# Choosing the early pass's tokens inside attention, and clamping and signing the weight words on ScalarE

## The chip, the cores and the metric

The kernel runs on one core of a Trainium2 chip, as one launch. The metric is the device time of that launch in microseconds (us). The engines are TensorE (PE, with its weight loads PEld), VectorE (DVE), ScalarE (ACT), GpSimd (POOL) and SyncE (SP); each runs its own list of instructions in order and waits on semaphores where another engine's result is needed.

## The reference, cut to what matters

Three layers follow each other on 2304 tokens of 512 features.

```
scores = q k^T / 8                       # 4 batches x 8 heads, 576 x 576, head size 64
keep scores >= max - tau, softmax, times v        -> x [2304, 512]
logits = x @ w_gate; e = argmax(logits)           # 8 experts, one for each token
out[tokens of e] = gate * relu(x @ w1[e]) @ w2[e] # 512 -> 1024 -> 512
h = out @ w_in;  result = (h - tanh(h)) @ w_out   # 512 -> 2048 -> 512
```

`w_in` and `w_out` arrive as float64, that is as pairs of 32-bit words; the kernel turns them into float32 by operations on the words.

## The kernel before, in words

**Attention** (class `Attn`). A unit is one head of two batches; there are 16 units of 9 steps, 144 steps, one step for 128 rows of scores. `run` writes the order by hand: the tables `PL`, `PFIRST` and `PLAST` give each job a step relative to its unit and one of four phases in the step, and `hooks` lets the next class put jobs at steps counted from the start of the last unit (step 135). In a step PE makes scores, VectorE takes the maximum (L235) and masks (L254), ScalarE takes the exponential (L241) and a half-precision copy (L262), and GpSimd the rest of the split (L266). SyncE then issues a DMA transpose for each three steps (L273), and PE multiplies by v (L298). SyncE also issues the loads of q, k and v (v: L107, L109) and the stores of finished rows. For each pair of heads PE transposes the rows (L557) and adds their part of the logits (L565), and VectorE sums it into `L` (L572, L574). The logits of the first half of the tokens are whole at step 95, those of the second half only after the last unit.

**The early pass.** To have work while the second half is finished, one pass of 240 tokens of the first half's most frequent expert is computed first. `best(0)` takes the argmax, `pick` counts by two matmuls (L609, L610), `pick2` finds the expert, `pick3` builds one-hot columns (9 of them at L653), `pick4` turns them into a table of rows by nine matmuls (L659), `pick5` takes those tokens out of the later lists. All of this stands at steps 9 to 15 of the last unit's count, after the last mask. `wearly` loads that expert's eight weight tiles (L1215), `gather_exp` fetches the 240 rows by two indirect DMAs from GpSimd's queue (L1280), `trans` transposes them on PE (L1239), and `evac` splits them into a high and a low part (L1249 on ScalarE, L1253 on VectorE).

**Routing and the expert passes** (`Mlp.run`, `route`, `plan`). After the last logits `route` sorts all tokens on VectorE, with the early pass's matmuls between its parts. Then come eight passes p = 1 to 8, one for each expert from the fullest-capacity table `CAPS`, of 8 steps each (steps g = 8 to 71). In a step PE makes one block of `h` (L1262), ScalarE applies relu (L1303), VectorE takes the low part (L1304), and two steps later PE multiplies by `w2` (L1323). The PSUM tile of `h` has two buffers. Each weight tile is loaded, cast on ScalarE (`wcast`, L1223) and its remainder taken on VectorE or GpSimd (`wlow`, L1227). `FIRST` names the tiles of pass 1 that are loaded and split before its steps begin.

**The words.** Beside the expert passes, 32 jobs `conv` turn half a tile of `w_in` or `w_out` each into float32 and store it in DRAM. `TB["conv"]` and `TB["cv"]` and the line in `plan` put the parts of job n at steps 8 + 14n/9 plus 0, 4, 5 and 6: `load`, `bits`, `sign`, `store`. `bits` shifts and joins the words on VectorE (L1385, L1387) and, in three jobs of four, compares with a threshold (L1390). `sign` takes the absolute value on ScalarE (L1397); in three jobs of four VectorE then makes the sign (L1401), in the fourth ScalarE makes two sign functions (L1395, L1396) and GpSimd adds them (L1399). GpSimd multiplies (L1403).

**The last layer** has 96 steps (g = 72 to 167) of two groups of matmuls (L1262, L1351) with the tanh expression on ScalarE, VectorE and GpSimd between them.

## Time and profile before

| | before |
|---|---|
| device time, median of 3 runs | 1088.42 us (1088.06 to 1088.99) |
| the profiled execution's own time | 1084.18 us |
| its span | 1081.9 us |
| PE busy | 960.4 us (89%) |
| PE weight loads busy | 871.8 us (81%) |
| VectorE busy | 922.6 us (85%) |
| ScalarE busy | 689.3 us (64%) |
| GpSimd busy | 751.2 us (69%) |
| mean granted TensorE clock | 0.949 of full speed |

Busy time counts an instruction from its start to its end, with any time that it is held up inside. A number in square brackets behind an instruction is the time that its engine was idle before it, with the instruction that ended the idle time. L12 is line 12 of the kernel file; a line can be a helper's.

### The profile page before, as it was taken

The page shows a single profiled execution, that of the slowest core. Times are in us where ns is not written, and L with a number is a line of the kernel's source. Part 1 is how long each engine was busy: PE and PEld are TensorE (multiplying, and loading weights), DVE is VectorE, ACT ScalarE, POOL GpSimd, SP SyncE. Part 2 cuts the span into 40 slices and gives each one's busy share as a digit, 9 for nine tenths or more (in the row PEclk, how much of TensorE's full clock was granted, in tenths as well). Part 3 has the DMA queues.
Part 4 walks back from the last instruction along what each step waited for, and adds up shares of the span by engine and source line. Part 5 has one row for each costly group of instructions (what it writes and reads, how often), then busy time and mean ns, then how long its engine had stood idle before and what let it go on. Part 6 is the DMA issues. An engine that isn't in the chain of part 4 may idle for free. (4 is left out here: it accounts for less than half of the span.)

```text
span 1081.9 us, 20819 instructions
## 1 busy us (share of the span) xinstructions
PE 960.4 (89%) x7349; PEld 871.8 (81%) x7349; DVE 922.6 (85%) x1663; ACT 689.3 (64%) x1284; POOL 751.2 (69%) x656
## 2 busy tenths in 40 slices
PE   4687987887986889999998879999999999999997
PEld 3576876776875888899997878788998989999886
DVE  5899888978996748989999986999988989889894
ACT  5797887987983435455555656676666566656662
POOL 3897886886875055466766677787767767677763
PEclk9698898998897789999999999999999999999999
DMA  6798998998899468778788876320101101000000
GB/s 159 149 218 161 206 209 157 216 210 159 158 171 237 155 196 267 252 258 276 259 282 280 267 247 199 95 76 11 49 8 37 30 20 40 8 30 1 21 10 30
DMA packets 250568, 157.29 MB, mean 145 GB/s; under 512 B 179754, under 2 KB 224188, under 8 KB 250461
## 3 DMA queue, kind: packets, MB, share of 16 engines
q1 hardware_dynamic: 246701, 145.18, 53.5%
q0 software_dynamic: 3312, 10.46, 2.8%
q8 instruction: 59, 0.97, 0.4%
q14 instruction: 48, 0.39, 0.1%
q10 hardware_dynamic: 448, 0.30, 0.1%
HBM read 89.24 MB, written 23.57 MB: 104 GB/s over the span
## 5 line engine op out<-in xcount | busy, mean ns | idle before, releaser
L266 POOL TENSOR_TENSOR e<-em,e 128x1024 f16<-128x1024 f32 (+1 forms) x98 | 158.4, 1617 | 55.8 <-ACT e L262 26.1
L1470 POOL TENSOR_SCALAR tm<-u 128x384 uint8<-128x384 f32 x88 | 129.7, 1474 | 50.7 <-ACT u L1466 50.2
L1262 PE MATMUL h<-xa,w 128*128 128x240 f32 (+6 forms) x816 | 135.7, 315 | 17.1 <-DVE w L1227 9.7
L1262 PEld LDWEIGHTS h<-xa,w 128*128 128x128 f32 x816 | 122.4, 194 | 23.4 <-DVE w L1227 11.6
L241 ACT ACTIVATE e<-sps,n 128x576 f32<-128x576 f32 x144 | 111.1, 771 | 34.3 <-DVE n L235 34.2
L1323 PE MATMUL y<-hbuf,w 128*128 128x240 f32 (+6 forms) x768 | 128.3, 317 | 1.0 <-ACT yo L1326 0.9
L1466 ACT ACTIVATE u<-h 128x384 f32<-128x384 f32 x96 | 47.2, 491 | 116.6 <-PE h L1262 116.4
L1473 DVE SCALAR_TENSOR_TENSOR w<-y,w 128x384 f32<-128x384 f32 x96 | 121.3, 1264 | 0.0
L1227 POOL TENSOR_TENSOR w<-raw,w 128x1024 fp32r<-128x1024 f32 x38 | 99.1, 2608 | 31.4 <-ACT w L1223 31.1
L254 DVE SCALAR_TENSOR_TENSOR em<-sps,n,e 128x576 f32<-128x576 f32 x144 | 116.7, 811 | 4.4 <-ACT e L241 2.9
L1323 PEld LDWEIGHTS y<-hbuf,w 128*128 128x128 f32 x768 | 115.3, 193 | 3.9 <-ACT yo L1326 1.6
L235 DVE TENSOR_REDUCE n<-sps 128x1 f32<-128x576 f32 x144 | 107.2, 744 | 11.1 <-PE sps L227 11.1
L1487 POOL TENSOR_TENSOR gl<-w,gh 128x384 fp32r<-128x384 f32 x83 | 85.4, 1029 | 37.1 <-ACT gh L1486 37.1
L1262 PE MATMUL h<-xk,w 128*128 128x384 f32 x576 | 108.5, 337 | 2.5 <-DVE w L1227 2.2
L1262 PEld LDWEIGHTS h<-xk,w 128*128 128x128 f32 x576 | 101.2, 188 | 7.2 <-DVE w L1227 2.9
L298 PE MATMUL ops<-vh,et 128*128 128x64 f16 (+1 forms) x2240 | 97.0, 201 | 9.9 <-DVE x L304 9.0
L262 ACT CAST e<-em 128x576 f16<-128x576 f32 x144 | 100.4, 698 | 3.0 <-DVE em L254 2.6
L298 PEld LDWEIGHTS <-et 128*128 128x128 f16 (+1 forms) x2240 | 83.3, 106 | 22.4 <-issue 18.7
L227 PE MATMUL sps<-ka,qa 128*128 128x288 f32 x320 | 86.3, 362 | 9.5 <-DVE em L254 5.4
L1223 ACT CAST w<-raw 128x1024 fp32r<-128x1024 f32 x80 | 83.7, 1052 | 15.1 <-DMA raw<-in_moe_w_dram 9.3
L1474 DVE SCALAR_TENSOR_TENSOR w<-y,w 128x384 f32<-128x384 f32 x96 | 79.6, 829 | 10.0
L1351 PE MATMUL y<-w,gh 128*128 128x512 f32 x258 | 81.6, 397 | 1.7 <-POOL w L1227 1.3
(271 smaller groups left out, 2345.7 us busy)
## 6 DMA issues: line engine op xcount, KB each, us to landing
raw<-in_moe_w_dram SPq DMA_DIRECT2D x72, 512.0 KB, 5.5
cv<-in_moe_w_in_dram SPq DMA_DIRECT2D x16, 512.0 KB, 4.8
cv<-in_moe_w_out_dram SPq DMA_DIRECT2D x16, 512.0 KB, 4.7
wscr<-cm SPq DMA_DIRECT2D x32, 256.0 KB, 2.6
raw<-wscr SPq DMA_DIRECT2D x16, 512.0 KB, 4.3
xw<-yT SPq DMA_DIRECT2D x24, 192.0 KB, 2.5
vv<-in_v_dram SPq DMA_DIRECT2D x8, 512.0 KB, 5.3
raw<-in_q_dram SPq DMA_DIRECT2D x6, 576.0 KB, 6.8
```

The lines of the kernel that those rows point to most:

```text
L227: nc.tensor.matmul(ps[:, c, 0:288], lhsT=w[:, o:o + 128], rhs=ka[:, j, 288 * c:288 * c + 288], start=(i == 0), stop=(i == n - 1))
L235: nc.vector.tensor_reduce(out=n[:, 0:1], in_=ps[:, :, 0:288], axis=AX.XY, op=ALU.max, negate=True)
L241: nc.scalar.activation(out=e, in_=ps[:, :, 0:288], func=AF.Exp, bias=n[:, 0:1])
L254: nc.vector.scalar_tensor_tensor(out=self.em[u, g][:, i].rearrange("p (a b) -> p a b", a=2), in0=ps[:, :, 0:288], scalar=n[:, 1:2], in1=e, ...
L262: self.nc.scalar.copy(self.e16[u, g][:, i, 0:S], self.em[u, g][:, i])
L266: eng.tensor_tensor(out=e16[:, r, S + 64:], in0=em[:, r, 0:512], in1=e16[:, r, 0:512], op=ALU.subtract)
L298: nc.tensor.matmul(o[q], lhsT=et[:, base + c, q], rhs=vh[:, a, j, c if c < 5 else c - 5, :], start=(n == 0), stop=(n == len(terms) - 1))
L1227: eng.tensor_tensor(out=l, in0=raw, in1=h.bitcast(F32), op=ALU.subtract)
L1262: self.nc.tensor.matmul(out, lhsT=a, rhs=b, start=(i == 0), stop=(i == len(parts) - 1))
L1323: nc.tensor.matmul(self.ys[d], lhsT=a[:, f % 2, s], rhs=b, start=(f == 0 and i == 0), stop=(f == 7 and i == 2))
L1470: nc.gpsimd.tensor_scalar(out=mk, in0=u, scalar1=RCUT * RCUT, scalar2=None, op0=ALU.is_gt)
L1473: V.scalar_tensor_tensor(out=w, in0=y, scalar=b, in1=w, op0=ALU.add, op1=ALU.mult)
```

## The change

Four things are edited.

1. The hooks `best`, `pick`, `pick2`, `pick3`, `pick4` and `pick5` move from steps 9 to 15 of the last unit to steps -40 to -34, that is steps 95 to 101 of attention. Their PSUM tiles come from attention's one transposing bank (tag `t`), their scratch from attention's SBUF pool; the nine one-hot columns become a job of their own (`pick3b`), the table is copied out of PSUM at once and its last addition (`pick6`) stays at step 12, in front of the gather, which moves from step 14 to 12. `x_exp` and `trans` of the early pass move from step 20 to 15, phase 1, `evac` from step 21 to 15, phase 2. `wearly` stays at step 11 and its eighth tile no longer takes a buffer of the tag `raw`.
2. `FIRST` gets a fourth tile, (2, 0).
3. In `conv` a new part `mag` at step 3 makes the sign of the high word (into a bfloat16 tile) and its absolute value in place, both on ScalarE. `bits` begins with a maximum against the threshold on VectorE, and its compare goes; the sign on VectorE (L1401) and the fourth job's sum on GpSimd (L1399) go. The absolute value of the joined word and GpSimd's product stay.
4. The two threshold constants of the old sign functions go.

```diff
     def pick2(self, T):
...
+        self.li1 = T([128, E, NH])
+        tt(self.li1, self.pre1, inc[:, :, 0:NH], ALU.add)
...
+    def pick4(self):
+        nc = self.nc
+        ps = self.attn.tp.tile([128, 512], F32, tag="t", name="pkt")[:, 0:2]
         for t in range(NH):
             nc.tensor.matmul(ps, lhsT=self.B1[:, t], rhs=self.R1[:, t], start=(t == 0), stop=(t == NH - 1))
+        self.idxf = self.cp.tile([128, 2], F32, name="idxf")
+        nc.vector.tensor_copy(self.idxf, ps)
+
+    def pick6(self):
         self.idx1 = self.cp.tile([128, 2], I32, name="idx1")
-        nc.vector.tensor_scalar(out=self.idx1, in0=ps, scalar1=float(ZR), scalar2=None, op0=ALU.add)
+        self.nc.vector.tensor_scalar(out=self.idx1, in0=self.idxf, scalar1=float(ZR), scalar2=None, op0=ALU.add)
...
-FIRST = [(0, 0), (1, 0), (0, 1)]
+FIRST = [(0, 0), (1, 0), (0, 1), (2, 0)]
...
-        return {(9, 0): [self.open1, lambda: self.best(0)],
-                (10, 2): [lambda: self.pick(self.psum)],
-                (11, 0): [lambda: self.pick2(T()), self.wearly],
-                (12, 0): [self.pick3],
-                (14, 2): [lambda: self.pick4(self.psum), lambda: [self.gather_exp(0, m, NE - 128 if m else 128) for m in range(2)]],
-                (15, 0): [self.pick5],
+        return {(9, 0): [self.open1],
+                (-40, 3): [lambda: self.best(0)],
+                (-39, 2): [self.pick, lambda: self.pick2(Carve(self.attn.one.tile([128, 1024], F32, name="pk")))],
+                (-38, 2): [self.pick3],
+                (-37, 2): [self.pick3b],
+                (-35, 2): [self.pick4],
+                (-34, 2): [self.pick5],
+                (11, 0): [self.wearly],
+                (12, 0): [self.pick6, lambda: [self.gather_exp(0, m, NE - 128 if m else 128) for m in range(2)]],
+                (15, 1): [lambda: self.x_exp(0), lambda: [self.trans(("e", 0, m), NE - 128 if m else 128) for m in range(2)]],
+                (15, 2): [lambda: [self.evac(("e", 0, m), 128 * m, NE - 128 if m else 128) for m in range(2)]],
                 (17, 0): [lambda: self.wcast(-1, 0, 0), lambda: self.wlow(-1, 0, 0, self.nc.gpsimd)],
-                (20, 1): [lambda: self.x_exp(0), lambda: [self.trans(("e", 0, m), NE - 128 if m else 128) for m in range(2)]],
                 (21, 0): [lambda: self.wcast(-1, 1, 0)],
-                (21, 1): [lambda: self.wlow(-1, 1, 0, self.nc.vector)],
-                (21, 2): [lambda: [self.evac(("e", 0, m), 128 * m, NE - 128 if m else 128) for m in range(2)]]}
+                (21, 1): [lambda: self.wlow(-1, 1, 0, self.nc.vector)]}
...
-                raw = sp.tile([128, 1024], F32, tag="we" if j and i < 3 else "raw", name="raw", bufs=4)
+                raw = sp.tile([128, 1024], F32, tag="we" if j else "raw", name="raw", bufs=4)
...
+        def mag():
+            st["sg"] = self.sp.tile([128, 512], BF16, tag="gh", name="sg", bufs=LY + 1)
+            nc.scalar.activation(out=st["sg"], in_=st["hf"], func=AF.Sign)
+            nc.scalar.activation(out=st["hf"], in_=st["hf"], func=AF.Abs)
+
         def bits():
             m = st["m"].bitcast(U32)
-            nc.vector.tensor_scalar(out=m, in0=st["hi"], scalar1=3, scalar2=0x40000000,
+            nc.vector.tensor_scalar(out=st["m"], in0=st["hf"], scalar1=T, scalar2=None, op0=ALU.max)
+            nc.vector.tensor_scalar(out=m, in0=m, scalar1=3, scalar2=0x40000000,
                                     op0=ALU.logical_shift_left, op1=ALU.bitwise_xor)
             nc.vector.scalar_tensor_tensor(out=st["lo"], in0=st["lo"], scalar=29, in1=m,
                                            op0=ALU.logical_shift_right, op1=ALU.bitwise_or)
-            if not sg:
-                nc.vector.tensor_scalar(out=st["m"], in0=st["hf"], scalar1=-T, scalar2=None, op0=ALU.is_le)
 
         def sign():
             c = st["lo"].bitcast(F32)
-            if sg:
-                nc.scalar.activation(out=st["m"], in_=st["hf"], func=AF.Sign, bias=self.tt2[:, 0:1])
-                nc.scalar.activation(out=st["hf"], in_=st["hf"], func=AF.Sign, bias=self.tt2[:, 1:2])
-            nc.scalar.activation(out=c, in_=c, func=AF.Abs, scale=0.5 if sg else 1.0)
-            if sg:
-                nc.gpsimd.tensor_tensor(out=st["m"], in0=st["m"], in1=st["hf"], op=ALU.add)
-            else:
-                nc.vector.scalar_tensor_tensor(out=st["m"], in0=st["hf"], scalar=T, in1=st["m"],
-                                               op0=ALU.is_ge, op1=ALU.subtract)
-            nc.gpsimd.tensor_tensor(out=st["m"], in0=st["lo"].bitcast(F32), in1=st["m"], op=ALU.mult)
+            nc.scalar.activation(out=c, in_=c, func=AF.Abs)
+
+        def mul():
+            nc.gpsimd.tensor_tensor(out=st["m"], in0=st["lo"].bitcast(F32), in1=st["sg"], op=ALU.mult)
...
-        return [load, bits, sign, store]
+        return [load, mag, bits, sign, mul, store]
...
-                  47, 51, 52, 54, 57, 57), "cv": (0, 4, 5, 6), "eng": "DPDPDPDPDPPDDDPP"}
+                  47, 51, 52, 54, 57, 57), "cv": (0, 3, 4, 5, 5, 6), "eng": "DPDPDPDPDPPDDDPP"}
```

The arithmetic before attention's end, the passes, the routing and the last layer are as they were.

## Rows read from the trace of the kernel before

**Rows 1.** Windows by stage: start:end, length, busy us of each engine, PEclk, DMA, GB/s
```profile
50.00:332.00 282.00, 230.94 (x3085) 205.15 (x3086) 250.39 (x647) 237.21 (x416) 232.51 (x235) 0.92 0.99 187
332.00:392.00 60.00, 49.77 (x455) 47.44 (x455) 37.39 (x123) 19.76 (x34) 18.92 (x20) 0.77 0.62 169
392.00:661.00 269.00, 245.08 (x1635) 233.41 (x1635) 234.40 (x296) 142.80 (x251) 171.38 (x96) 0.98 0.82 267
735.00:1011.00 276.00, 275.65 (x1381) 248.63 (x1381) 245.93 (x348) 171.07 (x360) 200.06 (x161) 1.00 0.07 23
```
**Rows 2.** Windows over attention around steps 95 to 101 and after them
```profile
228.40:239.60 11.20, 10.44 (x141) 9.31 (x141) 10.53 (x29) 11.12 (x21) 9.46 (x10) 0.89 1.09 199
245.10:332.00 86.90, 72.06 (x979) 64.12 (x980) 80.07 (x205) 72.75 (x126) 70.56 (x74) 0.91 0.89 166
```
**Rows 3.** Timeline, VectorE near steps 95 and 101: start, us, what, idle before it
```profile
228.40 0.22 DVE L574 TENSOR_TENSOR L<-L,ops 128x72 f32<-128x72 f32 x1
245.10 0.82 DVE L127 TENSOR_REDUCE pm<-vv 128x1 f32<-128x640 f32 x1 [5.51 <-DMA vv<-in_v_dram]
```
**Rows 4.** Sum over the four windows that hold the early choice on VectorE
```profile
sum 7.67, PE 6.23 PEld 6.02 DVE 7.03 ACT 2.29 POOL 1.53; mean PE 1.56 PEld 1.50 DVE 1.76 ACT 0.57 POOL 0.38
```
**Rows 5.** Timeline of the passage from attention to routing: all engines
```profile
332.07 0.81 DVE L254 SCALAR_TENSOR_TENSOR em<-sps,n,e 128x576 f32<-128x576 f32 x1
334.96 0.28 PE L609 MATMUL y<-O,onesh 128*128 128x152 f16 x1 [5.22 <-DVE O L578]
335.18 0.27 POOL L279 TENSOR_SCALAR su<-su,sc 128x9 f32<-128x9 f32 x1
344.35 2.99 PE L298 MATMUL ops<-vh,et 128*128 128x64 f16 x56
344.98 1.08 POOL L1280 DMA_INDIRECT xr<-rows,idx  x1 [9.53 <-DMA raw<-in_moe_w_dram]
352.83 0.66 PE L1239 MATMUL y<-ident,xr 128*128 128x128 f32 x4 [3.29 <-DMA xr<-rows,idx]
354.68 1.01 PE L1239 MATMUL y<-ident,xr 112*128 112x112 f32 x4 [1.19 <-DMA xr<-rows,idx]
359.92 0.23 DVE L574 TENSOR_TENSOR L<-L,ops 128x72 f32<-128x72 f32 x1 [2.88 <-PE ops L565]
390.37 4.31 PE L1262 MATMUL h<-xa,w 128*128 128x240 f32 x36 [0.45 <-ACT yo L1326]
```
**Rows 6.** Timeline at the start of pass 1: SyncE's loads, ScalarE's cast
```profile
393.59 1.19 SPq L1215 DMA_DIRECT2D raw<-in_moe_w_dram  x2
398.41 1.05 ACT L1223 CAST w<-raw 128x1024 fp32r<-128x1024 f32 x1 [4.67 <-DMA raw<-in_moe_w_dram]
```
**Rows 7.** Windows of pass 1, of passes 4 and 5, of passes 6 and 7
```profile
392.00:421.70 29.70, 25.26 (x186) 24.16 (x186) 20.45 (x48) 13.07 (x25) 13.13 (x8) 0.89 0.88 294
499.60:567.20 67.60, 64.02 (x430) 62.54 (x429) 65.33 (x80) 37.20 (x66) 44.77 (x27) 1.00 0.85 274
567.20:633.80 66.60, 55.23 (x406) 52.22 (x405) 62.23 (x64) 35.48 (x63) 45.09 (x25) 1.00 0.80 265
```
**Rows 8.** Groups of instructions, 392 to 660 us, VectorE: busy us, mean ns, idle before
```profile
L1401 DVE SCALAR_TENSOR_TENSOR cm<-cv,cm 128x512 f32<-128x512 f32 x24 | 31.0, 1292 | 0.0
L1304 DVE SCALAR_TENSOR_TENSOR hbuf<-h,hbuf 128x240 fp32r<-128x240 f32 (+6 forms) x64 | 30.9, 483 | 22.5 <-ACT hbuf L1303 22.3
L1390 DVE TENSOR_SCALAR cm<-cv 128x512 f32<-128x512 f32 x24 | 24.1, 1005 | 0.8
```
**Rows 9.** The same of ScalarE and GpSimd
```profile
L1396 ACT ACTIVATE cv<-cv,knt 128x512 f32<-128x512 f32 x8 | 6.2, 772 | 0.3
L1395 ACT ACTIVATE cm<-cv,knt 128x512 f32<-128x512 f32 x8 | 6.1, 767 | 10.8 <-DVE cv L1387 10.8
L1403 POOL TENSOR_TENSOR cm<-cv,cm 128x512 f32<-128x512 f32 x32 | 45.4, 1419 | 49.8 <-issue 11.4 <-ACT hbuf L1303 11.0 <-ACT w L1223 10.3
L1399 POOL TENSOR_TENSOR cm<-cm,cv 128x512 f32<-128x512 f32 x8 | 11.0, 1370 | 9.7 <-ACT cv L1396 9.7
```
**Rows 10.** Single lines: shortest, median, longest ns, first and last start
```profile
L1401 DVE SCALAR_TENSOR_TENSOR cm<-cv,cm x24: 676/684/3494, 411.9 to 618.6; 128x512 f32<-128x512 f32 x24
L1390 DVE TENSOR_SCALAR cm<-cv x24: 426/428/2800, 410.4 to 616.9; 128x512 f32<-128x512 f32 x24
```

More of the change, by code (lines that the diff above doesn't have):

```diff
@@ L604, in best, with pick @@
         tt(self.O[:, :, 1 + NH * P:1 + NH * P + NH], eq, bt(tm), ALU.is_equal)
-    def pick(self, psum):
+    def pick(self):
         nc = self.nc
-        self.tot1, self.pre1 = psum("y2", [128, E, NTL + 1]), psum("y3", [128, E, NH])
+        n = E * (NTL + 1)
+        t = self.attn.tp.tile([128, 512], F32, tag="t", name="pkp")
+        self.tot1 = t[:, 0:n].rearrange("p (e t) -> p e t", e=E)
+        self.pre1 = t[:, n:n + E * NH].rearrange("p (e t) -> p e t", e=E)
         nc.tensor.matmul(self.tot1, lhsT=self.onesh, rhs=self.O, start=True, stop=True)
@@ L633, in pick3 @@
         n9 = lambda dt=F32: T([128, NH], dt)
-        li, O1 = T([128, E, NH]), T([128, E, NH])
-        loc, loi, lo, h1, vl, tv = n9(I32), n9(I32), n9(), n9(), n9(), n9()
+        li, O1 = self.li1, T([128, E, NH])
+        loc, loi, lo, h1, tv = n9(I32), n9(I32), n9(), n9(), n9()
+        vl = self.cp.tile([128, NH], F32, name="vl")
         A, R, B = T([128, NH, 2]), T([128, NH, 2], F16), T([128, NH, 128], F16)
-        self.O1, self.loc1, self.vl, self.B1, self.R1 = O1, loc, vl, B, R
-        tt(li, self.pre1, self.inc1[:, :, 0:NH], ALU.add)
+        self.O1, self.loc1, self.vl, self.B1, self.R1, self.lo1 = O1, loc, vl, B, R, lo
         tt(O1, O, self.sel1.unsqueeze(2).to_broadcast([128, E, NH]), ALU.mult)
@@ L1073, in run @@
             nc.gpsimd.memset(self.ab[:, i:i + 1], self.kn[2 * i])
-        T = float(np.nextafter(np.float32(3.4332275390625e-05), np.float32(0)))
-        self.tt2 = self.cp.tile([128, 2], F32, name="knt")
-        for i in range(2):
-            nc.gpsimd.memset(self.tt2[:, i:i + 1], T if i else -T)
         self.keep = sp.tile([128, 3072], F32, tag="lxa", name="keep")
@@ L1368, in conv @@
         T = 3.4332275390625e-05
-        sg = n % 4 == 3
         st = {}
```

8 lines of the change are left out of this document (3 added, 5 removed).

## The prediction

> **What bounds the kernel now.** I read the windows by stage first [rows 1]. From 735 to 1011 us PE is busy 275.65 of 276 us at the full granted clock: the last layer is PE's own, and nothing in the change touches it, so it can only begin earlier or later. The reader should look for the stages where PE is not full. There are three. In attention (50 to 332) PE has 231 of 282 us, VectorE 250, ScalarE 237, GpSimd 233, and the DMA engines are at 0.99: everything is near full and VectorE is the fullest of the engines. In the passage from attention to the expert passes (332 to 392) no engine but PE is half busy, the granted clock is 0.77, and the stage is a chain of waits. In the expert passes (392 to 661) PE has 245 of 269.
>
> Second, the windows of single passes [rows 7]. In passes 4 and 5 PE idles 3.6 us of 67.6, in 6 and 7 it idles 11.4 of 66.6, and VectorE is busy 65.3 and 62.2: as the experts' capacity falls, a step of PE becomes shorter than VectorE's work beside it, and VectorE bounds. Pass 1 idles 4.4 of 29.7 with VectorE at only 20.5, so its reason is another.
>
> Third, the groups of instructions there [rows 8, 10]. L1390 takes 0.43 us at the median but 1.0 on the mean and 2.8 at the worst; L1401 0.68, 1.29 and 3.5. L1304, whose one big input lies in PSUM, has 0.48 on the mean for tiles of 240 and more. So much of VectorE's busy time is being held up, and only in instructions that work from SBUF, as GpSimd's do.
>
> Fourth, the timeline of the passage [rows 5]: who ends each idle time, from the last mask to pass 1.
>
> **The change part by part.**
>
> *The choice inside attention.* 39 VectorE instructions move to steps 95 to 101, and one copy is new. In the old place they fill four short windows of 7.67 us together with VectorE busy 7.03 [rows 4]. I price them at 7.67. New are waits of VectorE for the counting matmuls and for the table's nine, and of PE for the shared PSUM bank; the nearest row has VectorE idle 5.51 us for another result, but that is a DMA; PE's queue in attention is nearly full rather than late, so I allow 0 to 1.5 us. Behind these wait the step's mask and, through it, the split and the DMA transpose. The cover: VectorE is busy 10.53 of 11.20 us in the very steps [rows 2], so nothing hides there, but right behind, at step 101, it stands 5.51 us until the loads of v land [rows 3]. Those were issued behind a queue of transposes on SyncE, which the later masks do not reach yet, so they land when they did. 7.67 + 0.5 against 5.51 leaves 2.66; I take 2.5 us lost. Ends: 0 (all in the gap) and 9.2 (the loads move too). From 245 to 332 VectorE is busy 80 of 87 us [rows 2], so what is lost there is hardly made good.
>
> *The passage.* Removed: PE's 5.22 us for the argmax at L609 [rows 5]. It is not all gain. The next thing late is the last head's own chain: GpSimd's L279 at 335.2, which opens the reciprocal on VectorE, then the rows, and with them the PSUM half that PE needs for its next product. PE so gains some 2 us there. Then the gather: idx no longer waits for PE at 344, and GpSimd is free at 335.5, so it is issued some 8 us earlier, near 337. From the first issue to the first transposing took 352.83 - 344.98 = 7.9 us, so rows are there near 345 and 346. The transposes now stand ahead of the products of rows 4 to 8 in PE's order, where PE comes near 343.5: it waits some 2 us there in place of 3.29 + 1.19 later. After them come 84 products, for which 2.99 us for 56 [rows 5] give 4.5 us, and the 4.9 us of logits that stood behind the transposes before (355.0 to 359.9). So the sum of the logits, at 359.92 before, ends near 356: 4 us. Ends: 0 (gather as late as before, counted from the end of attention) and 9.7 (5.22 + 3.29 + 1.19). From that sum to pass 1's first matmul at 390.37 lies the sorting and its gather, 30.5 us, which I leave as they are.
>
> *wearly.* Its place in SyncE's queue is behind the last transpose as before, so its loads start where they did; the eighth no longer waits for a buffer and holds the rows' stores up less, which nobody waits for. Nothing.
>
> *The fourth FIRST tile.* At 393.59 SyncE issues pass 1's loads and ScalarE stands 4.67 us at the first cast with relu behind it [rows 6]. One load of 0.52 MB less in that crowd, at the 294 GB/s of [rows 7], is 1.8 us; its cast (1.05) and remainder go to the stage before, where ScalarE has 19.8 of 60 and VectorE 37.4 [rows 1]. I take 1.5; ends 0 and the stage's whole 4.4.
>
> *The words.* VectorE loses L1401, 24 times; L1390 becomes the maximum, of the same shape and strides, and comes 8 times more often. At mean durations 31.0 - 8 x 1.005 = 23.0 us; at the medians 24 x 0.684 - 8 x 0.428 = 13.0 [rows 8, 10]. GpSimd loses L1399, 11.0 us [rows 9]; its product reads a bfloat16 operand now and I leave it at 1.42. ScalarE gains two functions in 24 jobs, 24 x (0.767 + 0.772) = 36.9 us [rows 9]. The 32 jobs spread over 50 steps, 0.64 a step, so passes 4 to 7 (32 steps) hold 0.64 of all: VectorE 8.3 (medians) to 14.7 us (means), ScalarE +23.6. PE's idle there is 15.0 [rows 7]. ScalarE was busy 72.7 of 134 us in these passes and becomes 96.3 of some 125, so it has room; its new functions stand a step ahead of VectorE's maximum, with a relu between that VectorE needs anyway, so no new wait arises there. But relu can come behind them. I take 8 us, near the medians, and 1 for passes 1 to 3, where PE is nearly full. Ends: 14.7 + 2, and on the other side 14.7 - 23.6 = -9, if every added function stood ahead of a relu that PE waits for.
>
> The Trainium skill (SBUF — State Buffer, section SBUF: two separate sides) calls the port that VectorE and GpSimd share an exclusive lock, held for a whole instruction, against VectorE's two-port modes and its instructions with two SBUF inputs. The longest L1401, 3.5 us, agrees with it. By that rule each held-up time goes with its instruction and GpSimd's 11.0 us come back too, so the words would be worth 14.7 in passes 4 to 7 and up to PE's whole idle; without it 8.3. The full return is my first rival, priced from the rows alone.
>
> **Sum.** -4 + 2.5 - 1.5 - 9 = -12.0 us. The profiled execution took 1084.18 us (span 1081.9 and 2.3 around it), so it would be 1072.2; the median of the runs is 4.24 above the profiled one, and I put the forecast on the median: 1088.4 - 12.0 = 1076.4 us.
>
> **Rivals.**
>
> *A. VectorE gives all of it back.* Passes 4 to 7 lose PE's whole 15.0 us of idle, passes 1 to 3 another 2, the passage 7, pass 1's load 2.5, attention costs 1: -25.5, 1062.9 us. For it: idle before L1401 is 0.0, VectorE never rests [rows 8]. Against: DMA is at 0.80 to 0.85 there [rows 7] and ScalarE fills up.
>
> *B. Moved, not saved.* The choice costs attention its whole 9.2, the passage gives nothing, because the gather lands as late against PE as before; words and load give 9 of their 10.5: +0.2, 1088.6 us. For it: VectorE's 250 of 282 in attention [rows 1]. Against: the 5.51 us gap.
>
> *C. ScalarE's queue, the slower side.* In passes 4 to 7 relu waits behind sign and absolute value, the low part behind relu, and PE behind the low part, since `h` has two buffers. Each job then costs 1.54 us and gives back 0.7: -9 us of gain become 9 of loss, with 3 for the rest: +6, 1094.4 us. It decides once ScalarE's 1.54 us fall between the end of an `h` and its relu in more than about half of the jobs (then the 23.6 us outweigh VectorE's 8 to 15). For it: ScalarE already stands 10.8 us in 8 jobs at L1395 for VectorE [rows 9], and what stands behind stands too. Against: after the change sign comes ahead of the shift and waits only for the load. The Trainium skill (ScalarE: Activation LUTs, section Rules for kernel authors) advises VectorE, not ScalarE, for simple functions; the medians agree with that, 0.77 against 0.43 us for the same tile, and this is the rival that it would lead to.
>
> **How the numbers follow.** Forecast 0.55, A 0.14, B 0.13, C 0.13, and 0.05 for a loss elsewhere (a late tile, a slower first pass). A measurement of this kernel can tell about 0.2%, 2.2 us, from no change. Forecast and A are faster; B splits into 0.03, 0.07 and 0.03; C is slower, and of the rest 0.04. Faster 0.72, same 0.08, slower 0.20. The forecast's own range is 1066 to 1084. All lower ends together would give 1058, all upper ones 1107, which no one case reaches; for 8 in 10 I take 1063 (A) to 1091, which leaves out most of C.
>
> **What would show it.** Attention's last mask, at 332.1 us before [rows 5], 2 to 3 us later, with VectorE's wait for v shortened from 5.5 to under 1. No idle of PE at L609, the gather issued near 337 on the old clock, and pass 1's first matmul at 390.4 + 2.5 - 4 = 389 us. PE's idle in pass 1 near 3 us, in passes 6 and 7 near 5 instead of 11.4, and ScalarE near 0.75 busy there. The last layer's 276 us unchanged. I am wrong if the last mask moves by more than 6 us (B), or if relu's wait for PE's `h` shrinks to nothing while passes 6 and 7 are not shorter (C).

## The result and the profile after

| | before | after |
|---|---|---|
| device time, median of 5 runs each | 1088.06 us (1085.72 to 1088.99) | 1077.96 us (1075.77 to 1079.61) |
| ratio, after to before | | 0.9911, 95% interval 0.9889 to 0.9932 |
| span of the profiled execution | 1081.9 us | 1076.0 us |

The change makes the kernel 10.1 us faster; 12.0 had been forecast, and the forecast time of 1076.4 us lies 1.6 us below the median. The two traces differ by only 5.9 us of span, because the profiled execution of before, at 1084.18 us, was shorter than any of the timed ones (1085.08 to 1091.95 over all comparisons). A trace is one execution: where a difference of one or two microseconds matters, the medians and the experiments decide.

The windows of after that answer to [rows 1, 2, 7], in this order: from the last mask to the last logits, pass 1, passes 4 and 5, passes 6 and 7, the last layer, and in attention from VectorE's sum L574 to the first value tile L127 (columns as in [rows 1]):

```profile
338.42:358.20 19.78, 14.55 (x188) 13.69 (x189) 5.37 (x17) 6.45 (x12) 6.42 (x9) 0.65 1.06 269
390.70:419.10 28.40, 23.70 (x187) 23.06 (x186) 18.41 (x40) 16.67 (x33) 15.36 (x10) 0.94 0.83 282
496.30:560.10 63.80, 63.76 (x432) 62.59 (x431) 52.23 (x74) 46.45 (x82) 38.57 (x24) 1.00 0.87 285
560.10:623.80 63.70, 55.22 (x404) 51.99 (x404) 52.07 (x60) 40.39 (x75) 38.57 (x22) 1.00 0.83 275
729.10:1005.10 276.00, 276.00 (x1381) 249.54 (x1381) 245.02 (x347) 170.94 (x360) 198.18 (x160) 1.00 0.07 23
229.49:251.60 22.11, 16.21 (x152) 14.14 (x153) 21.49 (x68) 11.84 (x21) 10.35 (x11) 0.58 1.00 189
```

Read them against before. The passage took 359.92 - 332.07 = 27.9 us [rows 5] and takes 19.8. Passes 4 to 7 took 134.2 us [rows 7] and take 127.5; in them VectorE was busy 127.6 us and is busy 104.3. PE is now full in passes 4 and 5 and still idles 8.5 us in 6 and 7, where every other engine has room. The last layer is 276 us, as before. The stretch in attention took 245.10 - 228.40 = 16.7 us [rows 3] and takes 22.1. From relu to relu, passes 1 to 7 together went from 241.8 to 233.1 us; of what lies behind them, pass 8 is 2.7 us longer in this trace and the last layer as long as before.

**Attention.** The timeline of after, VectorE, in and behind the choice (columns as in [rows 3]):

```profile
231.06 2.12 DVE L578 TENSOR_TENSOR O<-rt 128x72 f16<-128x72 f32 x1
235.65 0.82 DVE L578 TENSOR_TENSOR pk<-pk 128x8 f32<-128x8 f32 x1
241.74 3.65 DVE L660 TENSOR_SCALAR pk<-i128h,pk 128x128 f16<-128x128 f16 x9
251.60 0.81 DVE L127 TENSOR_REDUCE pm<-vv 128x1 f32<-128x640 f32 x1
```

The window of the same stretch in before (columns as in [rows 1]):

```profile
228.40:245.10 16.70, 11.61 (x159) 10.26 (x158) 10.54 (x30) 11.93 (x22) 12.34 (x13) 0.91 1.11 205
```

Six masks (L254) fall into the stretch before and after, so the difference is the choice. VectorE was busy 10.54 us in it and is busy 21.49: the choice takes 10.95 us of VectorE here. 6.16 us of them are time in which VectorE stood before (16.70 - 10.54), 0.62 us of idle time are left, and the stretch is 5.41 us longer. The granted clock is 0.58 in it, 0.91 before; VectorE is full here, so no cost of that is seen.

The same stretch of GpSimd:

```profile
230.96 2.13 POOL L266 TENSOR_TENSOR e<-em,e 128x1024 f16<-128x1024 f32 x1 [2.04 <-ACT e L262]
235.26 1.20 POOL L266 TENSOR_TENSOR e<-em,e 128x512 f16<-128x512 f32 x1 [0.42 <-ACT e L262]
242.49 2.14 POOL L266 TENSOR_TENSOR e<-em,e 128x1024 f16<-128x1024 f32 x1 [5.77 <-DMA vv<-in_v_dram]
```

Lay the two over each other. O's write starts 0.10 us after a split of GpSimd and ends with it. Nine of the experiments below have this write in attention: in five no split lies beside it and it takes 0.24 us, in four a split does and it takes 1.8 to 1.9. The nine one-hot columns contain one that took 2.13 us, against a median of 0.25; it starts 0.06 us after GpSimd's split from 242.49 to 244.63 and ends with it. L127 no longer waits: the 5.51 us gap [rows 3] is used up whole.

The Trainium skill (SBUF — State Buffer, section SBUF: two separate sides) has it that of VectorE and GpSimd whichever starts first gets the port that they share, and that the loser is blocked for the other's whole instruction. These rows agree for the write of O, the one-hot column and the 128x8 instruction at 235.65: each starts behind a split and lasts until it ends. Not every instruction of VectorE is held up so: a reduction at 235.46 (L581, 128x1 from 128x8) takes 0.16 us inside the split that starts at 235.26.

**The passage.** The timeline of after that answers to [rows 5], all engines:

```profile
338.42 0.81 DVE L254 SCALAR_TENSOR_TENSOR em<-sps,n,e 128x576 f32<-128x576 f32 x1
341.54 0.28 POOL L279 TENSOR_SCALAR su<-su,sc 128x9 f32<-128x9 f32 x1
342.59 0.91 PE L298 MATMUL ops<-vh,et 128*128 128x64 f16 x14 [5.07 <-DVE x L304]
342.91 1.07 POOL L1289 DMA_INDIRECT xr<-rows,idx  x1 [1.10 <-DVE idx L673]
349.41 1.84 PE L1248 MATMUL y<-ident,xr 128*128 128x128 f32 x8
358.20 0.23 DVE L574 TENSOR_TENSOR L<-L,ops 128x72 f32<-128x72 f32 x1
389.01 4.28 PE L1271 MATMUL h<-xa,w 128*128 128x240 f32 x36 [0.49 <-ACT yo L1335]
```

PE no longer waits for the argmax. It waits instead 5.07 us for the rows L304, which stand behind the denominator L279 on GpSimd; for the first half of this time a DMA transpose is late too (a weight load of PE waits for it until 340.03). The gather goes out 4.5 us after the mask, where it was 12.9, and PE does eight transposes in one go, with no wait in front, where [rows 5] had 3.29 and 1.19.

The granted clock has a part in it. These are the windows of the last 18 logits products (L565) with three transposes among them, up to the last sum, before and after:

```profile
355.48:359.92 4.44, 4.44 (x24) 4.44 (x23) 0.69 (x2) 2.02 (x4) 0.00 (x0) 0.50 0.91 264
355.46:358.20 2.74, 2.66 (x22) 2.57 (x23) 1.23 (x2) 2.73 (x4) 0.47 (x3) 1.00 1.06 380
```

Before, PE had stood 3.29 and 1.19 us for the rows just ahead of them and did them at 1.2 GHz (0.50); after, it had not stood there and did them at 2.4 GHz (1.00), 1.70 us faster.

**The words.** Groups of after over 392 to 660 us, VectorE first (columns as in [rows 8]):

```profile
L1399 DVE TENSOR_SCALAR cm<-cm 128x512 uint32<-128x512 uint32 x32 | 39.2, 1224 | 1.1
L1398 DVE TENSOR_SCALAR cm<-cv 128x512 f32<-128x512 f32 x32 | 28.5, 891 | 0.6 <-issue 0.4 <-DMA wscr<-cm 0.2
L1401 DVE SCALAR_TENSOR_TENSOR cv<-cv,cm 128x512 uint32<-128x512 uint32 x32 | 28.2, 880 | 1.1
...
L1394 ACT ACTIVATE cv<-cv 128x512 f32<-128x512 f32 x32 | 21.7, 678 | 1.0
L1393 ACT ACTIVATE sg<-cv 128x512 bf16<-128x512 f32 x32 | 21.4, 669 | 0.0
```

L1399 is now the shift and L1398 the new maximum. Both are still held up: their means are 1.22 and 0.89 us, while their medians are 0.43 and 0.42 and the longest 2.66 and 2.47. The two functions on ScalarE take 0.67 us each, steadily. Who waits for whom in passes 6 and 7 of after (560 to 624 us), as waiter, what ended the wait, us in total, times, longest:

```profile
ACT cv L1406 <- DVE cv L1401: 21.5, 8, 4.2
...
PE h L1271 <- DVE hbuf L1313: 3.9, 4, 1.5
...
PE h L1271 <- DVE w L1236: 2.1, 5, 0.6
...
PE y L1332 <- ACT yo L1335: 1.5, 2, 0.8
```

The last three, with 0.5 us each in front of two transposes, are the whole 8.5 us for which PE stands in these passes: the low part of `h` and weight remainders on VectorE, and ScalarE's copies of finished blocks.

And one such place in the timeline, all engines but SyncE:

```profile
574.62 2.59 POOL L1236 TENSOR_TENSOR w<-raw,w 128x1024 fp32r<-128x1024 f32 x1
...
574.99 2.50 DVE L1399 TENSOR_SCALAR cm<-cm 128x512 uint32<-128x512 uint32 x1
...
577.52 0.69 DVE L1401 SCALAR_TENSOR_TENSOR cv<-cv,cm 128x512 uint32<-128x512 uint32 x1
578.13 0.45 DVE L1313 SCALAR_TENSOR_TENSOR hbuf<-h,hbuf 128x288 fp32r<-128x288 f32 x1
578.25 0.67 ACT L1406 ACTIVATE cv<-cv 128x512 f32<-128x512 f32 x1 [3.95 <-DVE cv L1401]
...
578.63 1.86 PE L1271 MATMUL h<-xa,w 128*128 128x288 f32 x12 [0.66 <-DVE hbuf L1313]
```

A split of GpSimd runs from 574.62 to 577.21. VectorE's shift beside it ends 0.28 us later, after 2.50 us where the median is 0.43; the join and then the low part of `h` follow in VectorE's order, and PE waits for that low part.

### The profile page after: what moved, and what is told of

It is laid out like the page before. It is cut to its first block, busy times and chain, and to the rows that moved or that the text cites. A ratio compares the mean times of both kernels' runs of the same rounds, so it can differ in the third digit from the quotient of the medians.

```text
span 1076.0 us, 20810 instructions
## 1 busy us (share of the span) xinstructions
PE 961.3 (89%) x7349; PEld 872.5 (81%) x7349; DVE 891.3 (83%) x1648; ACT 715.4 (66%) x1332; POOL 733.2 (68%) x646
## 4 chain that ended last, share of the span: by engine, by line
PE 42%; DVE 13%; issue 4%; ACT 3%; DMA 3%; POOL 2%; SPq 0%; POOLq 0%; DVEq 0%; ACTq 0%
PE h L1271 20%; PE y L1360 15%; PE y L1332 6%; DVE w L1479 2%; DVE w L1480 2%; DVE cm L1399 2%; DMA raw<-in_moe_w_dram 1%; DVE cm L1398 1%; DVE w L1236 1%; DVE w L1477 1%; ACT w L1232 1%; DMA wscr<-cm 1%; DVE cv L1401 1%; DVE tm L1478 1%; POOL w L1236 1%
## 5 line engine op out<-in xcount | busy, mean ns | idle before, releaser
L1236 POOL TENSOR_TENSOR w<-raw,w 128x1024 fp32r<-128x1024 f32 x38 | 95.2, 2507 | 73.9 <-ACT w L1232 45.5
L254 DVE SCALAR_TENSOR_TENSOR em<-sps,n,e 128x576 f32<-128x576 f32 x144 | 116.6, 810 | 5.2 <-ACT e L241 3.4
L1332 PEld LDWEIGHTS y<-hbuf,w 128*128 128x128 f32 x768 | 115.2, 193 | 5.4 <-ACT yo L1335 3.1
L235 DVE TENSOR_REDUCE n<-sps 128x1 f32<-128x576 f32 x144 | 107.0, 743 | 10.1 <-PE sps L227 10.0
L1480 DVE SCALAR_TENSOR_TENSOR w<-y,w 128x384 f32<-128x384 f32 x96 | 77.7, 809 | 10.7 <-DVE w L1479 0.9
```

The lines of the kernel that those rows point to most:

```text
L235: nc.vector.tensor_reduce(out=n[:, 0:1], in_=ps[:, :, 0:288], axis=AX.XY, op=ALU.max, negate=True)
L254: nc.vector.scalar_tensor_tensor(out=self.em[u, g][:, i].rearrange("p (a b) -> p a b", a=2), in0=ps[:, :, 0:288], scalar=n[:, 1:2], in1=e, ...
L1236: eng.tensor_tensor(out=l, in0=raw, in1=h.bitcast(F32), op=ALU.subtract)
L1332: nc.tensor.matmul(self.ys[d], lhsT=a[:, f % 2, s], rhs=b, start=(f == 0 and i == 0), stop=(f == 7 and i == 2))
```

## The experiments

Each kernel was timed beside the kernel before on the same chip; ratios are to that.

**The choice alone**: the change without its words and without the fourth FIRST tile.

```diff
-FIRST = [(0, 0), (1, 0), (0, 1), (2, 0)]
+FIRST = [(0, 0), (1, 0), (0, 1)]
 (and conv, its constants and "cv" as in the kernel before)
```

> The early choice moved into attention and the eight weight tiles' buffers as in the change; the words and FIRST as before. Read from the two traces: attention +6.35 us (last mask 332.07 to 338.42), the passage from the last mask to the second half's logits -8.07, so about -1.7 us, 1086 us against a before of 1088. Rival (the whole gain comes from the passage, and attention's later end is this execution's own slowness): -8 us, 1080. Second rival (attention pays more than the passage returns): 1089 or more. In its trace the last mask should come 6 us later than before and the nine one-hot columns of L653's group should take 3.6 us together in place of 1.55, with a write of O of 2 us or more.

Measured: 1084.46 us against 1088.93, ratio 0.9976 (0.9959 to 0.9994). The medians are 4.5 us apart; the ratio and its interval say some 2.6 us faster (0.7 to 4.5), which is near the theory. The passage takes 21.0 us, the stretch in attention 251.06 - 229.71 = 21.4, and passes 4 to 7 are as long as before (134.3). Of the signs in its trace the one-hot columns came (3.66 us); the long write of O did not, since no split lay beside it (0.24 us), and the last mask came 4.7 us later, not 6.

**The words alone**: the kernel before with the new `conv` and nothing else.

```diff
-        return [load, bits, sign, store]
+        return [load, mag, bits, sign, mul, store]
 (mag, bits, sign, mul and "cv" as in the changed kernel)
```

> The words' new parts alone; choice and FIRST as before. The theory (VectorE bounds passes 4 to 7, and what it and GpSimd no longer do comes back there): passes 4 to 7 shorter by 7 to 8 us, all else the same, so 1080 us against 1088. Rival (the gain of these passes needs the earlier start of pass 1 or the fourth FIRST tile): under 3 us. Rival (ScalarE's 37 us more cost passes 1 to 3 what 4 to 7 gain): no change, 1088.

Measured: 1078.28 us, ratio 0.9904 (0.9882 to 0.9926), 10.5 us faster. The whole change has 0.9911. So the words alone do as much as the change, and beside them the 2.6 us of the choice can't be seen: the parts do not add. Passes 4 to 7 of this kernel, to be set beside the two middle rows of after:

```profile
503.10:630.50 127.40, 119.04 (x833) 114.67 (x833) 103.99 (x133) 86.76 (x155) 77.28 (x45) 1.00 0.85 281
```

127.4 us, against 127.5 in the change, with the same busy times: the choice plays no part in the passes. This run also tells how far attention varies. Its attention is the kernel before's, line for line, and its last mask stands at 337.9 us, not at 332.1; 5.1 us of that are there already at L574 (233.53 against 228.40).

**FIRST with three tiles**: the change with that one edit undone.

```diff
-FIRST = [(0, 0), (1, 0), (0, 1), (2, 0)]
+FIRST = [(0, 0), (1, 0), (0, 1)]
```

> The changed kernel with three FIRST tiles in place of four. Theory: the fourth tile gives nothing, because in pass 1 PE then waits 3.9 us for the third gathered block of pass 2's rows instead: within 1 us of the changed kernel, 1078. Rival (my prediction's step): 1.5 us slower, 1079.5. Rival (the fourth tile is what made pass 1 longer): 2 us faster, 1076.

Measured: 1076.49 us, ratio 0.9900 (0.9875 to 0.9924); the change has 0.9911 (0.9889 to 0.9932). No difference that can be told. Pass 1 is 28.7 us with three tiles and 28.4 with four.

**ScalarE's new work twice**: sign and absolute value each made twice in all 32 jobs, with the same values.

```diff
+            nc.scalar.activation(out=st["sg"], in_=st["hf"], func=AF.Sign)
             nc.scalar.activation(out=st["sg"], in_=st["hf"], func=AF.Sign)
+            nc.scalar.activation(out=st["hf"], in_=st["hf"], func=AF.Abs)
             nc.scalar.activation(out=st["hf"], in_=st["hf"], func=AF.Abs)
```

> The changed kernel with the two new ScalarE functions of every job done twice (sign written twice, absolute value taken twice; the result stays): ScalarE gets another 32 x 1.36 = 43 us. Theory (ScalarE has room, at 46.9 of 65.7 us in passes 4 and 5 and 38.5 of 60.6 in 6 and 7): 0 to 6 us slower than the changed kernel, 1078 to 1084. Rival (relu stands behind the new functions and PE behind relu, so each function costs its length in passes 4 to 7): 0.64 x 43 = 28 us slower, 1106.

Measured: 1088.89 us, ratio 1.0010 (0.9990 to 1.0031), 10.9 us above the change. ScalarE's 32 x 1.35 = 43 us of extra work cost a quarter of their length, which neither the theory (0 to 6 us) nor the rival (28) had. In passes 4 to 7:

```profile
499.20:635.00 135.80, 120.75 (x828) 116.26 (x827) 101.10 (x133) 109.87 (x192) 75.44 (x45) 0.97 0.80 264
```

with VectorE's wait for relu grown from 19.1 to 30.1 us, and PE's for ScalarE's copies from 1.5 to 4.2:

```profile
DVE hbuf L1313 <- ACT hbuf L1312: 30.1, 17, 3.3
...
PE y L1332 <- ACT yo L1335: 4.2, 2, 2.2
```

ScalarE is busy 23.0 us more there and the passes are 8.3 us longer, although ScalarE would seem to have had 127.5 - 86.9 = 40.6 us to spare. So the room was smaller than its busy share said. Relu does stand behind the new functions, as rival C had it; but that is not where PE waits. PE idles 15.1 us in these passes, 6.5 more than in the change, and its wait for the low part behind relu is 2.8 us, not more than the 3.9 of the change. What grew is its wait for the copies (by 2.7), for weight tiles, which ScalarE casts first (2.5), and in front of transposes (2.2). At the change's own dose the price of all this stays below what VectorE gives back.

**GpSimd's product twice**: the last product of each job made twice.

```diff
             nc.gpsimd.tensor_tensor(out=st["m"], in0=st["lo"].bitcast(F32), in1=st["sg"], op=ALU.mult)
+            nc.gpsimd.tensor_tensor(out=st["m"], in0=st["lo"].bitcast(F32), in1=st["sg"], op=ALU.mult)
```

> The changed kernel with GpSimd's product of every word job done twice (the result stays): GpSimd gets another 32 x 1.4 = 45 us, 29 of them in passes 4 to 7, where it is busy 76 of 126 us and has room. Theory (VectorE is held up while GpSimd reads SBUF, so what GpSimd does costs VectorE): VectorE's busy time in these passes grows by 10 to 25 us and the kernel takes 8 to 20 us more, 1086 to 1098. Rival (the two run side by side and only instruction lengths of VectorE itself count): 0 to 2 us, 1078 to 1080.

Measured: 1094.78 us, ratio 1.0063 (1.0042 to 1.0084), some 16.8 us above the change for 32 x 1.43 = 46 us more on GpSimd. Passes 4 to 7:

```profile
500.20:637.20 137.00, 120.25 (x833) 115.83 (x832) 115.22 (x133) 86.88 (x156) 106.73 (x66) 0.99 0.82 262
```

The three instructions of the jobs on VectorE, in the same passes:

```profile
L1398 DVE TENSOR_SCALAR cm<-cv 128x512 f32<-128x512 f32 x19 | 25.4, 1335 | 1.6 <-issue 1.4
L1399 DVE TENSOR_SCALAR cm<-cm 128x512 uint32<-128x512 uint32 x19 | 25.3, 1331 | 0.7
...
L1401 DVE SCALAR_TENSOR_TENSOR cv<-cv,cm 128x512 uint32<-128x512 uint32 x19 | 21.1, 1109 | 0.7
```

Nothing was added to VectorE, and it is busy 10.9 us longer (104.3 to 115.2). The three groups together took 63.1 us in the change (19.2, 27.7 and 16.2) and take 71.8. The passes are 9.5 us longer. GpSimd itself is not full, 107 of 137 us. The rival, that a job's product lies beside other work and costs nothing, falls. VectorE is one of two ways in which the product is paid for:

```profile
PE h L1271 <- DVE hbuf L1313: 8.2, 6, 2.5
...
PE t L1248 <- DMA xr<-rows,idx: 4.9, 2, 2.9
```

PE idles 8.2 us more than in the change. Its wait for VectorE's low part grew by 4.3 us, and a wait for gathered rows of 4.9 us is new: GpSimd issues those gathers, in its own order behind the doubled product (for pass 6 at 564.47, 3.2 us ahead of that pass's first relu, where the change has 4.5). So this run shows the hold-up on VectorE, but it does not price it alone.

**The one-hots back behind attention**: everything else of the change kept.

```diff
-        return {(9, 0): [self.open1],
+        return {(8, 3): [self.pick3b],
+                (10, 3): [self.pick5, self.pick4],
...
-                (-37, 2): [self.pick3b],
-                (-35, 2): [self.pick4],
-                (-34, 2): [self.pick5],
-                (11, 0): [self.wearly],
+                (11, 0): [self.open1, self.wearly],
```

> The changed kernel with the one-hot columns (pick3b), the table's matmuls (pick4) and pick5 back behind the last mask, where VectorE and PE stand idle for 2.6 and 5.1 us; argmax, counts and pick3 stay in attention, and the weight tiles' pool opens two steps later. Theory (in attention these cost 3.6 + 0.2 + 1.0 us of VectorE, held up by GpSimd, with nothing to hide them): attention's steps 95 to 102 go from 24.1 back to 19.5 to 20.5 us, the passage stays at 20 to 21: 4 us faster than the changed kernel, 1074. Rival (the cost is the wait for the counting matmuls and the argmax, which stay): under 1 us faster. Rival (PE is late behind the table in the passage): attention 4 us faster, passage 3 us slower, 1077.

Measured: 1074.08 us against 1088.07, ratio 0.9859 (0.9838 to 0.9879), 3.9 us faster than the change, and with the version "Both" below the best of those that were timed. The same stretch of attention (L574 to L127):

```profile
234.41:252.18 17.77, 13.77 (x143) 11.89 (x144) 16.68 (x51) 10.84 (x20) 9.57 (x10) 0.73 0.94 200
```

17.8 us, 4.3 less than in the change and near before's 16.7, though the first half of the choice is still in it. In the passage the one-hots come right behind the last mask:

```profile
338.54 2.83 DVE L660 TENSOR_SCALAR pk<-i128h,pk 128x128 f16<-128x128 f16 x9
...
340.93 0.34 POOL L279 TENSOR_SCALAR su<-su,sc 128x9 f32<-128x9 f32 x1
```

They lie in the time in which PE and VectorE wait for L279 anyway; the passage takes 21.1 us.

**Pass 2's last gather one step earlier**, on the change. In its trace PE stands 3.86 us in pass 1 for the third gathered block of pass 2, whose DMA is issued on GpSimd behind a split that waits for ScalarE.

```diff
-                at(max(g - B["ga"], 8) + m, self.gather_exp, p, m, w)
+                at(max(g - B["ga"], 8) + (min(m, 1) if p == 2 else m), self.gather_exp, p, m, w)
```

> The changed kernel with the third and fourth gathers of pass 2's rows issued by GpSimd one and two steps earlier, ahead of the remainder of a weight tile that GpSimd waits 9.7 us for. Theory (with the fourth FIRST tile in place, PE's 3.9 us wait for these rows in pass 1 is what comes next): pass 1 goes from 28.4 to about 25 us, 3 us faster in all, 1075. Rival (the weight tiles' loads are what pass 1 waits for in any case): under 1 us.

Measured: 1079.86 us, ratio 0.9900 (0.9871 to 0.9928). The wait is gone, and pass 1 is 27.9 us instead of 28.4: what comes next is late as well. No difference can be told in the whole time.

**Both, with the last denominator earlier as well**: the two edits above and `"de": (9, 1)` in `PLAST`, which lets GpSimd sum the last unit's denominator sooner.

```diff
-    PLAST = {"te": (4, 3), ..., "rc": (11, 1), ...
+    PLAST = {"te": (4, 3), ..., "de": (9, 1), "rc": (11, 1), ...
```

> late_onehot and gather_ahead together, and the last head's denominators (L279) on GpSimd one phase earlier, ahead of the last split instead of behind it. Theory: 4 us from attention, 3 from pass 1, and 2 from the passage, since the reciprocal and with it PE's next product wait for L279 at 341.5 with GpSimd idle before: 1069 us. Rival (the parts do not add, since pass 1 then waits for its weight loads): 1073.

Measured: 1072.41 us, ratio 0.9858 (0.9836 to 0.9881), the same as with the one-hots alone, and near the rival's 1073. The third edit was not timed by itself; the timeline says why nothing is seen of it. L279 now runs from 336.01 to 336.35, while VectorE is in the one-hots (L660, from 335.28) until 338.11 and takes the reciprocal only at 339.05. One wait has taken the place of another.

**The absolute value of the joined word one step later**, on the change and on the version with the late one-hots. It is meant to tell ScalarE's queue from VectorE's order, as what still holds PE up in passes 6 and 7.

```diff
-                  47, 51, 52, 54, 57, 57), "cv": (0, 3, 4, 5, 5, 6), "eng": "DPDPDPDPDPPDDDPP"}
+                  47, 51, 52, 54, 57, 57), "cv": (0, 3, 4, 6, 6, 7), "eng": "DPDPDPDPDPPDDDPP"}
```

> The changed kernel with the last absolute value, GpSimd's product and the store of every conversion job one step later; nothing else moves. In passes 4 to 7 of the changed kernel ScalarE stands 25.8 us in 12 places at L1406 for VectorE's join L1401, with relu, sign and casts queued behind, and PE still idles 8.5 us in passes 6 and 7. Theory S (ScalarE's queue sets those idle times): with the step between, ScalarE's wait shrinks to under 8 us, relu is earlier, PE's idle in passes 6 and 7 falls to under 4 us and the time by 4 to 8 us: 1070 to 1074, ratio to before 0.983 to 0.987. Theory V (VectorE's own order sets them: its sum L1313, which PE waits for, stands behind the shift L1399, which takes 2.50 us instead of 0.4 while GpSimd splits): ScalarE's wait shrinks as well, but PE's idle stays within 2 us of 8.5 and the time within 2.5 us of the changed kernel: 1075 to 1080, ratio 0.989 to 0.994.

> The same shift on the version whose one-hots stand after the last mask. By theory S it takes another 4 to 8 us off that version's 1074.1: 1066 to 1070, ratio to before 0.980 to 0.983. By theory V it stays within 2.5 us: 1072 to 1077, ratio 0.984 to 0.989.

Measured: 1078.11 us against 1086.89, ratio 0.9920 (0.9904 to 0.9936), on the change; 1075.77 us, ratio 0.9902 (0.9887 to 0.9917), with the late one-hots, in time within theory V's range and by its ratio a little above it, so nothing gained. On the change ScalarE's wait fell as meant, but a new one arose, since the job's one buffer `cm` is stored a step later (waits from 498 to 625 us):

```profile
DVE cm L1398 <- DMA wscr<-cm: 28.5, 11, 5.5
...
PE h L1271 <- DVE hbuf L1313: 9.5, 6, 2.8
...
ACT cv L1406 <- DVE cv L1401: 7.9, 6, 1.6
```

In passes 4 to 7 PE's wait for VectorE's low part grew from 3.9 to 9.5 us although ScalarE's for the join went from 25.8 to 7.9. By that kernel's windows PE idles 67.60 - 63.77 = 3.8 us in passes 4 and 5 and 62.00 - 55.15 = 6.9 in 6 and 7, 10.7 together; in the change it is 8.5. That speaks against ScalarE's wait at L1406 as the cause, and the time fits VectorE's order; but since the edit brought a wait of VectorE of its own, it does not prove it. This pair also bears on the late one-hots: here they are worth 2.3 us (1078.11 against 1075.77, with intervals that overlap), where they had gained 3.9. So their worth is known only as some 2 to 6 us (by the ratios, 0.0018 and 0.0052).

## Why the prediction was right, step by step

**The total** was right, 12.0 us forecast and 10.1 measured, and the forecast's case is the one that came. Its four terms were not equally good, and that they came so near in sum is in part luck: the words alone measured 10.5.

**The choice inside attention: 2.5 us lost forecast, about 5 measured.** The stretch L574 to L127 takes 16.7 and 15.9 us in the two kernels without the choice and 20.7 to 22.1 in the seven with the whole of it, so it grew by 4.0 to 6.2. "7.67 + 0.5 against 5.51" had the right form: the gap was there and was used up whole. What failed is the term of 7.67 us. Part of it is the reading: the windows that hold these instructions in before's timeline (332.80:334.90, 335.28:336.75, 337.87:341.39 and 344.52:345.64) come to 8.21 us with VectorE busy 7.65. The larger part is the place: in attention they take 10.95 us of VectorE. The windows after attention, where GpSimd does little (1.53 us of 7.67 in [rows 4]), could not show what a split beside them costs. The one-hots, 3.65 us in place of 1.55, and the write of O, 2.12 in place of 0.96, are the largest of it. Moving the one-hots and the small remainder back returned 4.3 us of the stretch. That they take 2.83 us there too, and that this costs little, is the point about place: time beside a wait is nearly free.

**The mark of rival B was met.** The prediction said that it would be wrong if the last mask moved by more than 6 us; it moved by 6.35. By the two traces 1.09 us of this lie ahead of the stretch (L574 at 229.49 against 228.40), 5.41 in it, and -0.15 behind it (338.42 - 251.60 = 86.82 us against 332.07 - 245.10 = 86.97). So the mark told rightly that the choice costs attention twice what was forecast. It is not a safe mark: in the kernel with the words alone, whose attention is unchanged, the mask came 5.82 us later than in before's trace, of which 5.13 lie ahead of the stretch. The length of the stretch tells the cost; the absolute time of the mask does not. B itself falls: its passage gives nothing, the measured one gives more than attention lost.

**The passage: 4 us forecast, 8.1 by the two traces.** The gather went out 336.6 on the old clock (342.91 - 6.35), where 337 was forecast; PE came to the transposes at 343.1 (349.41 - 6.35), where 343.5 was forecast; and the wait that takes the place of the argmax is the one named, the last head's L279. The step that failed is "it waits some 2 us there". It took the rows' 7.9 us from the first issue to the first transposing over from before; in the change the second block landed 5.2 us after its issue (8.3 in before), and PE did not wait. Why is open: over the seven kernels with the whole choice the landing took 5.2 to 8.9 us. The granted clock of the logits behind it, 1.00 where before had 0.50, is not in the forecast at all.

Followed along PE, the 8.1 us are made up so. The two waits for rows are gone, 4.5 us. 23 products and transposes that stood behind the argmax in PE's order, from 335.11 to 338.01 in before, are done before the mask, 2.9. (The window of before [rows 5] has 222 instructions of PE, that of after 188; the other 11 are the choice's own. The kernel with the words alone has a mask as late as the change's and 222 again, so the cause is the place of L609 and not the late mask.) The clock gives 1.7, the choice's own matmuls 0.4. Against that PE starts again 4.17 us behind the mask and not 2.89, 1.3 lost. The rest is 0.2.

How much of this is the execution? From the start to the last logits it was 359.9 us in before and 365.7 with the words alone; with the whole choice inside it was 358.2 in the change and 356.4 to 358.4 in four more kernels, but 361.6 and 364.8 in two others (the absolute value later, the gather earlier). In the last of these the passage took 26.0 us: its rows landed 7.5 and 8.9 us after their issue, PE waited 0.88 and 1.62 us in front of the transposes, much as forecast, and the last logits again took 4.54 us at a granted clock of 0.50. With the one-hots behind attention it was 355.3 to 358.9. The time of the choice alone, -2.6 us (-4.5 to -0.7), is the measure of the pair; -1.5 had been forecast. Two mis-sized terms cancelled in part, which is luck.

**wearly and the fourth FIRST tile: 0 and 1.5 us forecast, none measurable.** Pass 1's idle was forecast near 3 us and is 28.40 - 23.70 = 4.7, where it was 4.4. The step that failed is that a load less in the crowd would shorten PE's idle. With three tiles, in the trace of that experiment, PE waits 3.4 us in pass 1 for weight tiles (2.1 for remainders on VectorE, 1.3 for a cast on ScalarE); with four it waits for none of these, but 3.86 us for rows of pass 2, which were late as well:

```profile
396.80 1.05 ACT L1232 CAST w<-raw 128x1024 fp32r<-128x1024 f32 x1 [4.45 <-DMA raw<-in_moe_w_dram]
...
407.24 1.09 PE L1248 MATMUL t<-ident,xr 128*128 128x128 f32 x4 [3.86 <-DMA xr<-rows,idx]
```

The 4.67 us of ScalarE in [rows 6] are now 4.45, one tile later. So a wait for a load stands there with either number of tiles; why it does was not taken further.

**The words: 9 us forecast, 10.5 measured by the words alone, 6.7 of them in passes 4 to 7 by the trace, where 8 were forecast.** (Of the rest the trace of the words alone shows 0.6 us in passes 1 to 3; where the remainder lies is not shown.) VectorE gave back more than forecast, 23.3 us of busy time in these passes against 8 to 15. By the durations there, the sign's 20.2 us are gone (14 instructions of 1.44 on the mean). VectorE's weight remainders fell from 27.0 to 21.3 us. But the instructions of the jobs that stayed were not held up less in sum: shift, join and compare cost 60.7 us, and shift, join and maximum cost 63.1, with the maximum made in all 19 jobs and the compare in 14. The join's mean fell from 1.75 to 0.85 us and the shift's rose from 0.64 to 1.46: the hold-up moved from one to the other.

In this rival A had VectorE right, and PE's share wrong: PE got back 15.0 - 8.5 = 6.5 us of its idle, not 15.0. What PE waited for in passes 4 to 7 of before:

```profile
PE h L1262 <- DVE hbuf L1304: 5.1, 7, 1.4
...
PE h L1262 <- DVE w L1227: 4.3, 4, 1.6
...
PE t L1239 <- DMA xr<-rows,idx: 1.8, 2, 1.1
```

Two more waits of PE, 2.9 us, have no releaser in the profile; both end 0.1 us after VectorE has taken the low part of the gathered block before (L1253). The low part of `h` now costs PE 3.9 us, the remainders 2.1, the rows nothing. So most of what PE got back had been VectorE's. Part of it, the 1.8 us for rows whose gathers GpSimd issues, may be GpSimd's, which lost its sum in the same edit; no version leaves out that sum alone. PE is full in passes 4 and 5 now; in 6 and 7, where near 5 us of idle had been forecast, 8.5 are left. ScalarE was to be busy 96.3 us and is at 86.9, in part since the functions take 0.67 us and not 0.77; the rows that they were priced by, L1395 and L1396 [rows 9], read a second input (`knt`), which the new ones do not.

The Trainium skill (ScalarE: Activation LUTs, section Rules for kernel authors) prefers VectorE to ScalarE for relu, max, min, add and mul. Per instruction this case agrees for the maximum, 0.42 us at the median against 0.67 for the new functions of ScalarE on the same tile. For the kernel the move of the sign to ScalarE measured 10.5 us faster. VectorE's means in before, 1.00 us for the compare and 1.29 for the sign [rows 8], are what the comparison has to be made with.

**Rival C** did not decide, as forecast. It had the right engine, though: doubling ScalarE's part turned the whole gain of the change into nothing (1.0010). Its path is not shown: even then PE's wait for the low part behind relu was no longer than in the change.

**What stays open.** What would give back the last 8.5 us of PE's idle in passes 6 and 7 is not settled: the waits are listed above, but no edit removed one of them alone. The earlier use of VectorE for `h`, ahead of the shift, was not tried. Why the choice's gain is not seen beside the words' was not followed. Why attention's last mask varies by 6 us between executions of the same attention code was not followed either; pass 8 took 30.0 us in the change's trace and 27.1 to 29.2 in the others, and no cause was found that belongs to the change.

## What to carry to other kernels

Price an instruction that moves by its duration in the new place, beside the engine that works there, and not by its duration where it came from; and look for a place where its own engine waits anyway. Where two engines hold each other up, judge a move between engines by mean durations under load, for the whole group of instructions that stays and not for one, since the hold-up moves among them; and expect the gain to end at the next chain of waits, not at the sum of the time freed. An engine that shows a third of its time idle can still have little room, if something urgent stands behind its new work in order. Look for that in what the bounding engine waits for, not in the longest wait of any engine.

## What the runs showed of the hardware that was not expected

- GpSimd's work has a price that no busy share of GpSimd shows: 46 us more of it, in 32 products, lengthened the kernel by 16.8 us while GpSimd stayed at 107 of 137 us in passes 4 to 7. There VectorE was busy 10.9 us longer with the same instructions, and PE waited 4.9 us for rows whose gathers GpSimd issued behind the products.
- Some short instructions of VectorE take the length of the split beside them: a 128x72 write took 2.12 us instead of 0.24, one one-hot column 2.13 instead of 0.25, each beside a split of 2.1 us. In four of nine further traces the same write was held up so, in five it met no split.
- The same logits at the end of the passage took 4.44 us at a granted clock of 0.50, where PE had stood 3.29 and 1.19 us shortly before, and 2.74 at 1.00, where it had not.
- Of 23.3 us that VectorE got back in passes 4 to 7, 6.7 reached the time; of 23.0 us put on ScalarE there by the doubled functions, 8.3 did.
